# Weight conversions from the 24th step, batch 0's token mixer in four pieces, one matmul over zeros a step, and only batch 1 projected unsplit

## The chip, the cores and the metric

The kernel runs on one NeuronCore of one Trainium2 chip. The metric is the time that the device needs for one execution, in microseconds (us). Of several executions the median is taken. The engines are called PE (matrix multiplication), DVE (vector), ACT (scalar, activations), POOL (GpSimd) and SP, whose queue issues the DMAs.

## The reference

A linear attention with random features, over 8 batches, 8 heads, 576 tokens and 64 values a head, and behind it a mixer over tokens (rank 32) and a two-layer mixer over channels (512 to 2048 to 512). U, V and the two channel weights come as 64-bit floats.

```python
def phi(x):
    proj = np.einsum('bhsd,df->bhsf', x, w_phi)
    proj = proj - np.max(np.abs(proj), axis=-1, keepdims=True)
    return np.concatenate([np.exp(proj), np.exp(-proj)], axis=-1)
q_p, k_p = (phi(q), phi(k))
kv = np.einsum('bhsf,bhsd->bhfd', k_p, v)
z = np.sum(k_p, axis=2)
num = np.einsum('bhsf,bhfd->bhsd', q_p, kv)
den = np.einsum('bhsf,bhf->bhs', q_p, z)[..., None] + 1e-06
x = (num / den)                         # then (batch, seq, 512)

h = x.transpose(0, 2, 1) @ U @ V
u = x + h.transpose(0, 2, 1)
ch = np.maximum(u @ w_ch1, 0.0) @ w_ch2
return (u + ch).astype(np.float32)
```

## The kernel before, in words

**Attention by pairs.** A `Pair` is two heads of one batch, so there are 32 pairs, four to a batch. For each one k and q come in by DMA (`raw`, and the last 64 of the 576 tokens in `t_r`), PE transposes them (L282, L291), then k is projected in two halves (`project_k`), q in two halves (`project_q`), and the 64 last tokens apart (`project_k_tail`, `project_q_tail`). The features are two exponentials (L325, L326 for k; L337, L338 for q, whose maximum over partitions is taken on POOL, L335). `kv_tail` and `kv_main` build the sums over tokens in PSUM (L404, L411), L417 copies them out, `out_tail` and `out_main` multiply by q's features (L437, L450) and `normalize` divides (L424 to L429).

**Two ways to project.** An unsplit pair (`self.split` false; batches 0 and 1) multiplies 32-bit floats, each such matmul being two instructions on PE, and ACT copies the transposed tiles out (L300, L310). A split pair (batches 2 to 7) writes each number as a rounded high part and a rest: ACT casts the high part (L273), DVE subtracts for the rest (L274), PE multiplies in the faster format (L371, L394, L395), and for k the two results are added with a copy on ACT (L374) and an addition on DVE (L375).

**Mixers.** `Tokens` mixes over tokens: `split` (ACT L507, DVE L508) writes x as two parts, `down` multiplies by U (L521) into `pst`, `up` multiplies by V (L537) and adds to x (L538). A `Mixer` then handles 512 tokens: `transposes` (L553, parts on ACT L231 and DVE L232), and for each of 16 blocks f of the hidden layer `hidden(f)` (12 matmuls, L565, one PSUM bank, then `h_hi` on ACT L570 and `h_lo` on DVE L571) and `add(f)` (12 matmuls, L582). These 32 calls of a batch are its chunks. There is one mixer a batch, and a ninth for the 64 last tokens of all batches.

**Weights.** The 16 blocks of each channel weight are loaded as 64-bit words and converted, block by block, in `convert` (L137, L138, L140 on ACT; L141, L142 on DVE; a 64-bit integer addition on POOL, L146; scratch tile `w_ab`), then split into two parts (L223 on ACT, L224 on DVE). There are 32 such blocks: block 2f is of the first weight, 2f+1 of the second.

**The order.** The Python loop runs one pair behind the other, and a scheduler at build time may move instructions within what dependences allow. `step(fn)` issues one stage of a pair and then calls `pace.step()`: it counts the steps, issues the conversions that are due (`CONVERT`: from the first number on, all 32 by the second), and then either one piece of the first token mixer (`pieces`), or the share of mixer chunks that is due, or, while there are no chunks, two matmuls over zeros that keep PE going (`keep_busy`). Batch 0 fills the first 33 steps. Its pieces are made in `first_tokens`; after the last piece the 28 chunks (32 less `HELD`) are spread over the steps up to `BATCH`. `LOADS` says up to which block the words are loaded at each of the first seven pairs; these DMAs stand in SP's queue.

PSUM has three banks for the tag `at`, one for `ph` and four for `o`. In batch 0 the tiles that are asked for as `late` use the four banks of `o`; the unsplit `project_k` is among them, the split one uses `at`.

Of the kernel before, what the change touches and what calls it, by code (L numbers as in the profile page):

```python
# [25 lines left out]
def tile_kernel(  # L26
# [12 lines left out]
    nc = tc.nc  # L39
# [166 lines left out]
    def convert_block(i):  # L206
        f, n = divmod(i, 2)
        r = convert(words[f][n], f"w{n + 1}_{f}")
        if f < LAST:
            w = home.tile([P, 2, C], F32R, tag=f"w{n + 1}_{f}", name=f"w{n + 1}_{f}")  # L210
            split_w(r, w)
        elif n == 0:
            found[f] = r
            return
        else:
            w1_w, w = place(f, F32R, (2, C), f"w_{f}")
            split_w(found[f], w1_w)
            split_w(r, w)
            w1_t[f] = w1_w
        (w1_t, w2_t)[n][f] = w  # L220

    def split_w(r, w):
        nc.scalar.copy(out=w[:, 0, :], in_=r)  # L223
        nc.vector.tensor_sub(w[:, 1, :], r, f32(w[:, 0, :]))  # L224

    def w1_part(f, part, c):
# [5 lines left out]
        nc.vector.tensor_sub(dst_lo, src, f32(dst_hi))  # L232


    SPLIT = 2

    class Pair:


        def __init__(self, b, j):  # L240
            self.b, self.h0, self.nm = b, 2 * j, f"{b}_{j}"
            self.split = b >= SPLIT
            self.tail = slice((b % 2) * ST, (b % 2 + 1) * ST)
            nm, hs = self.nm, slice(self.h0, self.h0 + 2)
            self.raw = []
            for n, src in enumerate((k, q)):
                m = raw.tile([P, 2, NT // 2, 2 * D], F32, tag="raw", bufs=2, name=f"raw{nm}_{n}")
                self.loaded = nc.sync.dma_start(
                    out=m.rearrange("p h s e -> p h (s e)"),
                    in_=src[b, hs, 0:SM, :].rearrange("h (p t) d -> p h (t d)", t=NT))  # L250
                self.raw.append(m)

            self.t_r = raw.tile([P, 2 * D], F32, tag="t_r", bufs=1, name=f"t_r{nm}")
            for n, src in enumerate((k, q)):
                nc.sync.dma_start(
                    out=self.t_r[n * ST:(n + 1) * ST, :].rearrange("r (h d) -> r h d", h=2),
                    in_=src[b, hs, SM:S, :].rearrange("h r d -> r h d"))
# [388 lines left out]
    class Pace:  # L646
# [5 lines left out]
        def step(self):  # L652

            steps[0] += 1
            blocks((steps[0] - CONVERT[0]) * 2 * NFC // (CONVERT[1] - CONVERT[0]))
            if pieces:
                pieces.pop(0)()
                if not pieces:
                    self.chunks, self.steps = 32 - HELD, BATCH - steps[0]
                return  # L660
            n = (self.at + 1) * self.chunks // self.steps - self.at * self.chunks // self.steps
            self.at += 1
            mix(n)
            if not self.chunks:

                keep_busy(2, True)

# [3 lines left out]
    def keep_busy(n, here=False):  # L673
        wp = ps("busy", "ph")
        for _ in range(n):
            ins = nc.tensor.matmul(wp, zeros[:, 0:P], zeros, start=True, stop=True)
            if here:
                tc.keep_in_program_order(ins)

    LOADS = (1, 3, 6, 9, 12, 14, 15)  # L680
    CONVERT = (12, 62)
    BATCH = 67
    pieces = []
    HELD = 4
# [42 lines left out]
    def first_tokens(tk):  # L727
        m = []

        def begin():  # L730
            tk.up(2)
            tk.up(3)
            m.append(Mixer(tk.b, tk.x))
            m[0].transposes(0)

        def end():
            m[0].transposes(3)
            todo.extend(m[0].chunks())

        return [  # L740
            lambda: tk.split(1),
            lambda: tk.down(1),
            lambda: [tk.up(t) for t in range(2)],
            begin,
            lambda: [m[0].transposes(1), tk.up(NT)],
            lambda: m[0].transposes(2),
            end]

    if True:
        cur = Pair(0, 0)  # L750
        load_w_phi()
        cur.load_v()
        keep_busy(6)
        cur.transposes()
        cur.s_project_k0()
        cur.s_project_k1()
        cur.s_project_q0()
        nxt = Pair(0, 1)
        nxt.load_v()
        nxt.transposes()  # L760
        cur.s_kv0_q1()
        cur.s_kv1()
        x = home.tile([P, NT, C], F32, tag="w_last", name="x0")
        xt = moe.tile([P, C], F32, tag="xt", name="xt0")
        nc.vector.memset(xt[ST:P], 0.0)
        tk = Tokens(0, x, xt)
        for n, (b, j) in enumerate(pairs):

            far = Pair(*pairs[n + 2]) if n + 2 < len(pairs) else None
            if n < len(LOADS):  # L770

                with tc.issue_after(far.loaded.ins):
                    weights(LOADS[n])
            if far is not None:
                far.load_v()
            if nxt is not None:
                step(nxt.s_project_k0)
            step(cur.s_out0, x, xt)
            if nxt is not None:
                step(nxt.s_project_k1)  # L780
            step(cur.s_out1, x)
            if j == 1:
                tk.split(0)
            if j == NPAIR - 1:
                fill = []
                if nxt is not None:
                    fill = [nxt.s_project_q0, far.transposes, nxt.s_kv0_q1, nxt.s_kv1]
                if b == 0:
                    pieces.extend(first_tokens(tk))
                    for fn in fill:  # L790
                        step(fn)
                else:
                    tokens(tk, fill)
                    pace = Pace(32 - HELD, 34)
                if nxt is not None:
                    if b % 2 == 1:
                        xt = moe.tile([P, C], F32, tag="xt", name=f"xt{b + 1}")
                        nc.vector.memset(xt[ST:P], 0.0)
                    x = moe.tile([P, NT, C], F32, tag="x", name=f"x{b + 1}")
                    tk = Tokens(b + 1, x, xt)  # L800
            else:
                step(nxt.s_project_q0)
                if n == 0:
                    load_uv()
                if j == 1:
                    step(tk.down, 0)
                if far is not None:
                    step(far.transposes)
                step(nxt.s_kv0_q1)
                step(nxt.s_kv1)  # L810
            cur, nxt = nxt, far
        mix(len(todo) - HELD)
        x = moe.tile([P, NT, C], F32, tag="x", name="x_tail")
        nc.sync.dma_start(out=x, in_=u_dram[B])
        m = Mixer(B, x)
        for t in range(NT):
            m.transposes(t)
            mix()
        todo.extend(m.chunks())
        mix(len(todo))  # L820
# [31 lines left out]
```

## Time and profile before

| | |
|---|---|
| time, median of 3 runs | 1282.24 us (1282.2 to 1285.5) |
| the profiled execution | 1287.0 us, span of its instructions 1285.2 us |
| PE | 1252.3 us busy, 97% of the span |
| DVE | 643.4 us, 50% |
| ACT | 548.1 us, 43% |
| POOL | 202.9 us, 16% |

"Busy" is the time in which at least one instruction of the engine runs. The page's strip of the span in 40 slices shows where the engines differ: the shares of DVE and ACT are highest in the first seven slices (some 220 us), and the granted clock of PE is below full there alone.

```profile
DVE  5887665464555454555456455545455543211211
ACT  6788584444443444344343444344434431111110
PEclk9986899999999999999999999999999999999999
```

Five events of DVE mark the stages of the text below. A row of the timeline has the start, the time that the instructions took, the engine, line, operation, tiles, count, and in brackets the idle time before and what ended it.

```profile
94.98 0.76 DVE L508 TENSOR_TENSOR xs<-x,xs 128x256 fp32r<-128x256 f32 x2 [1.19 <-ACT xs L507]
...
122.04 0.68 DVE L232 TENSOR_TENSOR uT_lo<-pt,uT_hi 128x512 fp32r<-128x512 f32 x1
...
140.53 0.69 DVE L571 SCALAR_TENSOR_TENSOR h_lo<-ph,h_hi 128x512 fp32r<-128x512 f32 x1 [0.83 <-ACT h_hi L570]
...
181.18 0.69 DVE L571 SCALAR_TENSOR_TENSOR h_lo<-ph,h_hi 128x512 fp32r<-128x512 f32 x1
...
210.69 0.69 DVE L571 SCALAR_TENSOR_TENSOR h_lo<-ph,h_hi 128x512 fp32r<-128x512 f32 x1 [2.19 <-ACT h_hi L570]
```

The first is the start of the split of batch 0's last half of x, the second the last part of its transposed tokens, then come the 2nd, the 6th and the 9th `h_lo` of its mixer.

### The profile page before, as it was taken

What the parts mean: (1) busy time and instruction counts of PE and PEld (TensorE: products, weight loads), DVE (VectorE), ACT (ScalarE), POOL (GpSimd) and SP (SyncE); (2) the same over time, 40 slices, a digit from 0 to 9 for tenths busy, and PEclk for the clock granted to TensorE, in tenths of its full rate; (3) what the DMA queues carried; (4) which work ended last, traced back from release to release, by engine and by line L of the source; (5) the groups of instructions that cost most, each with busy time, mean ns of one, the idle gap of its engine ahead of it and who ended that gap; (6) DMA issues with size and microseconds to landing.
All of it is one profiled execution on the core that took longest, in us unless ns stands there. A gap on an engine that the chain in (4) does not pass through costs nothing.

```text
span 1285.2 us, 17973 instructions
## 1 busy us (share of the span) xinstructions
PE 1252.3 (97%) x6961; PEld 1071.5 (83%) x6968; DVE 643.4 (50%) x1425; ACT 548.1 (43%) x1167; POOL 202.9 (16%) x154
## 2 busy tenths in 40 slices
PE   9878999999999999999999999999999999999997
PEld 7656878888888888888888888888888888788886
DVE  5887665464555454555456455545455543211211
ACT  6788584444443444344343444344434431111110
POOL 3444352011110111111111111011111120000000
PEclk9986899999999999999999999999999999999999
DMA  6644321121113111210112111311121002100001
GB/s 192 204 140 148 93 61 35 50 76 27 30 47 111 28 29 45 78 61 25 47 47 75 28 30 47 111 29 28 45 77 61 21 1 86 66 1 1 33 1 33
DMA packets 90100, 75.38 MB, mean 59 GB/s; under 512 B 51488, under 2 KB 76448, under 8 KB 89888
## 3 DMA queue, kind: packets, MB, share of 16 engines
q1 hardware_dynamic: 90016, 74.24, 18.9%
q8 instruction: 55, 0.90, 0.3%
q14 instruction: 29, 0.24, 0.1%
HBM read 55.35 MB, written 18.87 MB: 58 GB/s over the span
## 4 chain that ended last, share of the span: by engine, by line
PE 89%; ACT 5%; DVE 3%; DMA 1%; issue 1%; SPq 0%; POOL 0%; DVEq 0%; ACTq 0%; POOLq 0%
PE o L582 30%; PE ph L565 30%; PE xp L450 8%; PE kv_ps L411 8%; PE T L291 2%; PE pk L371 2%; PE pp L521 1%; PE pt L553 1%; PE pq L394 1%; ACT w_ab L137 1%; PE kv_ps L404 1%; ACT w_ab L138 1%; PE xpt L437 1%; PE pq L395 1%; ACT w_ab L140 1%
## 5 line engine op out<-in xcount | busy, mean ns | idle before, releaser
L565 PE MATMUL ph<-uT_hi,w 128*128 128x512 f32 x1152 | 388.5, 396 | 1.1 <-ACT uT_hi L231 1.1
L582 PE MATMUL o<-w,h_hi 128*128 128x512 f32 x1152 | 330.4, 399 | 0.1
L565 PEld LDWEIGHTS ph<-uT_hi,w 128*128 128x128 f32 x1152 | 216.3, 189 | 44.7 <-ACT uT_hi L231 1.6
L582 PEld LDWEIGHTS o<-w,h_hi 128*128 128x128 f32 x1152 | 213.3, 190 | 41.9 <-issue 0.7
L571 DVE SCALAR_TENSOR_TENSOR h_lo<-ph,h_hi 128x512 fp32r<-128x512 f32 x144 | 99.2, 689 | 273.2 <-ACT h_hi L570 272.7
L565 PE MATMUL ph<-uT_lo,w 128*128 128x512 f32 x576 | 227.2, 394 | 0.5 <-DVE uT_lo L232 0.5
L570 ACT ACTIVATE h_hi<-ph 128x512 fp32r<-128x512 f32 x144 | 86.1, 598 | 323.4 <-PE ph L565 313.9
L582 PE MATMUL o<-w,h_lo 128*128 128x512 f32 x576 | 191.1, 396 | 0.0
L335 POOL PARTITION_ALL_REDUCE qp<-qp x64 | 128.1, 2002 | 386.4 <-ACT qp L334 375.2
L450 PEld LDWEIGHTS xp<-kv,qp 128*128 128x128 f32 x1024 | 125.7, 196 | 15.4 <-ACT qp L337 4.7
L450 PE MATMUL xp<-kv,qp 128*128 128x65 f32 x1024 | 127.1, 277 | 8.9 <-ACT qp L337 4.0
L565 PEld LDWEIGHTS ph<-uT_lo,w 128*128 128x128 f32 x576 | 108.7, 189 | 23.7 <-DVE uT_lo L232 2.6
L411 PEld LDWEIGHTS kv_ps<-vb,kp 128*128 128x128 f32 x1024 | 124.4, 196 | 3.6 <-issue 0.8
L411 PE MATMUL kv_ps<-vb,kp 128*128 128x65 f32 x1024 | 124.2, 276 | 0.1
L582 PEld LDWEIGHTS o<-w,h_lo 128*128 128x128 f32 x576 | 106.5, 188 | 20.9 <-issue 0.2
L274 DVE TENSOR_TENSOR T<-T,T 64x512 fp32r<-64x512 f32 x96 | 66.2, 689 | 84.7 <-ACT T L273 83.6
L273 ACT CAST T<-T 64x512 fp32r<-64x512 f32 x96 | 55.8, 581 | 97.8 <-PE pq L395 71.9
L335 POOL PARTITION_ALL_REDUCE qp_t<-qp_t x32 | 25.4, 794 | 381.0 <-ACT qp_t L334 380.8
L374 ACT COPY kp<-pk 128x256 f32<-128x256 f32 x96 | 35.6, 371 | 71.6 <-PE pk L371 71.4
L325 ACT ACTIVATE kp<-kp 128x512 f32<-128x512 f32 x64 | 40.4, 631 | 58.5 <-DVE kp L322 46.3
L375 DVE TENSOR_TENSOR kp<-pk,kp 128x256 f32<-128x256 f32 x96 | 40.2, 419 | 29.8 <-ACT kp L374 29.5
L336 DVE TENSOR_TENSOR qp<-qp 128x512 f32<-128x512 f32 x64 | 47.4, 740 | 11.6 <-POOL qp L335 11.0
(125 smaller groups left out, 1397.5 us busy)
## 6 DMA issues: line engine op xcount, KB each, us to landing
words<-in_moe_w_ch_dram SPq DMA_DIRECT2D x32, 512.0 KB, 6.7
raw<-in_k_dram SPq DMA_DIRECT2D x32, 256.0 KB, 2.8
raw<-in_q_dram SPq DMA_DIRECT2D x32, 256.0 KB, 3.0
vb<-in_v_dram SPq DMA_DIRECT2D x64, 128.0 KB, 2.6
u_dram<-x SPq DMA_DIRECT2D x32, 256.0 KB, 2.5
st<-u_dram SPq DMA_DIRECT2D x16, 512.0 KB, 4.4
out_dram<-st SPq DMA_DIRECT2D x32, 256.0 KB, 2.6
t_r<-in_k_dram SPq DMA_DIRECT2D x32, 32.0 KB, 2.2
```

Source lines behind the costliest of these rows:

```text
L273: nc.scalar.copy(out=dst[0:D], in_=src)
L274: nc.vector.tensor_sub(dst[D:2 * D], src, f32(dst[0:D]))
L325: nc.scalar.activation(out=kp[:, :, 0:F], in_=kp[:, :, F:2 * F], func=AF.Exp)
L335: nc.gpsimd.partition_all_reduce(qp[:, 0, :], qp[:, 1, :], P, ReduceOp.absmax)
L336: nc.vector.tensor_sub(qp[:, 1, :], qp[:, 1, :], qp[:, 0, :])
L375: nc.vector.tensor_tensor(out=k_w[:, ts_, :], in0=pk[:, :, 0, :], in1=kp[:, ts_, 0:F], op=ALU.add)
L411: nc.tensor.matmul(self.kv_v[:, f, g, :], kp[:, t, f * F:(f + 1) * F], self.vb[:, g, t, :], start=False, stop=(t == NT - 1), skip_group_ch ...
L450: nc.tensor.matmul(xv[:, c, :], qp[:, f, c * P:(c + 1) * P], self.kv[:, f, c // 2, :], start=(f == 0), stop=(f == 1))
L565: nc.tensor.matmul(ph, w1_part(f, l, c), r[:, c, :], start=(n == 0), stop=(n == 3 * NCC - 1))
L570: nc.scalar.activation(out=h_hi, in_=ph, func=AF.Relu)
L571: nc.vector.scalar_tensor_tensor(out=h_lo, in0=ph, scalar=0.0, in1=f32(h_hi), op0=ALU.max, op1=ALU.subtract)
L582: nc.tensor.matmul(self.o[t], l[:, cs], w2_t[f][:, r, :], start=(f == 0 and n == 0), stop=(f == NFC - 1 and n == 2))
```

## The change

Five things change. `CONVERT` goes from (12, 62) to (24, 63), and `LOADS` loads the words a pair later. The high part of the second weight's blocks is cast on DVE in place of ACT. `first_tokens` returns four pieces in place of seven, and the first of them is issued at once, ahead of the next step, so that the chunks start four steps earlier and are spread over 35 steps in place of 31. `keep_busy` is called for one matmul in place of two, and now also between the pieces. Batch 0 is projected split, so that batch 1 alone stays unsplit.

```diff
         if f < LAST:
             w = home.tile([P, 2, C], F32R, tag=f"w{n + 1}_{f}", name=f"w{n + 1}_{f}")
-            split_w(r, w)
+            split_w((nc.scalar.copy, nc.vector.tensor_copy)[n], r, w)
...
-            split_w(found[f], w1_w)
-            split_w(r, w)
+            split_w(nc.scalar.copy, found[f], w1_w)
+            split_w(nc.vector.tensor_copy, r, w)
...
-    def split_w(r, w):
-        nc.scalar.copy(out=w[:, 0, :], in_=r)
+    def split_w(copy, r, w):
+        copy(out=w[:, 0, :], in_=r)
         nc.vector.tensor_sub(w[:, 1, :], r, f32(w[:, 0, :]))
...
-    SPLIT = 2
+    UNSPLIT = 1
...
-            self.split = b >= SPLIT
+            self.split = b != UNSPLIT
...
                 if not pieces:
                     self.chunks, self.steps = 32 - HELD, BATCH - steps[0]
+                else:
+                    keep_busy(1, True)
                 return
...
             if not self.chunks:
-                keep_busy(2, True)
+                keep_busy(1, True)
...
-    LOADS = (1, 3, 6, 9, 12, 14, 15)
-    CONVERT = (12, 62)
+    LOADS = (-1, 1, 3, 6, 9, 12, LAST)
+    CONVERT = (24, 63)
...
             lambda: tk.split(1),
-            lambda: tk.down(1),
-            lambda: [tk.up(t) for t in range(2)],
-            begin,
-            lambda: [m[0].transposes(1), tk.up(NT)],
-            lambda: m[0].transposes(2),
-            end]
+            lambda: [tk.down(1)] + [tk.up(t) for t in range(2)],
+            lambda: [begin(), m[0].transposes(1), tk.up(NT)],
+            lambda: [m[0].transposes(2), end()]]
...
                     pieces.extend(first_tokens(tk))
+                    pieces.pop(0)()
```

Line numbers behind the edits are one higher in the changed kernel from L233 on, and three higher from about L670 on. Three places of the built order show what moves.

On DVE, from the copy of the second pair's sums (`kv_1`) on, the third pair's k is projected (`pk`, `kp`; `mk` is the maximum). Before:

```order
L417 COPY kv_1_483<-kv_ps_1_453 128x260
L142 TENSOR_SCALAR v_ab<-v_ab 128x64
L320 TENSOR_REDUCE mk_2_0_519<-pk_0_2_515 128x4
L322 TENSOR_TENSOR kp_2_0_518<-pk_0_2_515,mk_2_0_519 128x4x128
L336 TENSOR_TENSOR qp_1_1_466<-qp_1_1_466 128x512
```

Now:

```order
L418 COPY kv_1_525<-kv_ps_1_495 128x260
L321 TENSOR_REDUCE mk_2_t<-pkt_2_548 128x1
L337 TENSOR_TENSOR qp_1_1_509<-qp_1_1_509 128x512
L323 TENSOR_TENSOR kp_2_t<-pkt_2_548,mk_2_t 128x128
L376 TENSOR_TENSOR kp_2_0_557<-pk_0_2_558,kp_2_0_557 128x2x128
L376 TENSOR_TENSOR kp_2_0_557<-pk_0_2_563,kp_2_0_557 128x2x128
L321 TENSOR_REDUCE mk_2_0_568<-kp_2_0_557 128x4
```

The two additions of the split projection (L376) stand ahead of the maximum, each on a PSUM tile of its own, where before the maximum read PSUM at once.

On ACT, behind the last exponential of the third pair's first half of q, the conversions of the weights (`w_1_ab` and on; `words` are what was loaded) stood in a block ahead of the fourth pair's features. Before:

```order
L338 ACTIVATE qp_2_0_605<-qp_2_0_605 128x512
L137 ACTIVATE w_1_ab<-words_1_276 128x512
L138 ACTIVATE w_1_ab<-words_1_276 128x512
L140 ACTIVATE w_1_ab<-words_1_276 128x512
L524 CAST pst_614<-pp_0_615 128x256
L137 ACTIVATE w_1_ab<-words_2_277 128x512
L138 ACTIVATE w_1_ab<-words_2_277 128x512
L140 ACTIVATE w_1_ab<-words_2_277 128x512
L137 ACTIVATE w_2_ab<-words_1_495 128x512
L138 ACTIVATE w_2_ab<-words_1_495 128x512
L140 ACTIVATE w_2_ab<-words_1_495 128x512
L325 ACTIVATE kp_3_t<-kp_3_t 128x128
```

Now:

```order
L339 ACTIVATE qp_2_0_659<-qp_2_0_659 128x512
L375 COPY kp_3_0_774<-pk_0_3_775 128x2x128
L326 ACTIVATE kp_3_t<-kp_3_t 128x128
L375 COPY kp_3_0_774<-pk_0_3_780 128x2x128
L327 ACTIVATE kp_3_t<-kp_3_t 128x128
L375 COPY kp_3_1_818<-pk_0_3_819 128x2x128
L375 COPY kp_3_1_818<-pk_0_3_824 128x2x128
```

The fourth pair's features follow at once, with the copies of the split projection (L375) among them.

On DVE, from the eighth `h_lo` of the first mixer on, before:

```order
L571 SCALAR_TENSOR_TENSOR h_lo_7_1943<-ph_7_1929,h_hi_7_1942 128x512
L424 TENSOR_SCALAR den_2_1_1994<-xp_1_2_1985 128x4
L336 TENSOR_TENSOR qp_3_t<-qp_3_t 128x128
L425 RECIPROCAL den_2_1_1994<-den_2_1_1994 128x4
L429 TENSOR_TENSOR x_1208<-xp_1_2_1985,den_2_1_1994 128x2x2x64
L274 TENSOR_TENSOR tail_T_0_2047<-tT_0_2045,tail_T_0_2047 64x2x64 x2
L571 SCALAR_TENSOR_TENSOR h_lo_8_2012<-ph_8_1998,h_hi_8_2011 128x512
```

Now, the rows from a little behind the eighth up to the ninth:

```order
L141 TENSOR_SCALAR w_14_ab<-w_14_ab 128x512
L430 TENSOR_TENSOR xt_295<-xpt_2_1979,den_2_t_1986 64x64
L430 TENSOR_TENSOR x_1253<-xp_1_2_1990,den_2_0_1999 128x2x2x64
L142 TENSOR_SCALAR w_14_ab<-w_14_ab 128x512
L141 TENSOR_SCALAR w_15_ab<-w_15_ab 128x512
L142 TENSOR_SCALAR w_15_ab<-w_15_ab 128x512
L224 TENSOR_TENSOR w_14_2311<-w_14_ab,w_14_2311 128x512
L321 TENSOR_REDUCE mk_3_1_2024<-pk_1_3_2020 128x4
L223 CAST w_14_2363<-w_14_ab 128x512
L572 SCALAR_TENSOR_TENSOR h_lo_8_2017<-ph_8_2003,h_hi_8_2016 128x512
```

Before, the conversions were over by the eighth `h_lo`; now those of the last blocks stand behind it, the cast of a second weight's block (L223) among them.

## The prediction

> **What bounds the kernel now.** I read the windows view first, cut where the first batch hands over to its mixer (the five DVE rows stand in the section on the profile): at 95.0 us the split of the last half of x begins (the 6th `xs` subtraction, L508), at 122.0 the fourth `uT_lo` stands (L232), at 140.5, 181.2 and 210.7 the 2nd, 6th and 9th `h_lo` (L571) of the first mixer. A row gives the stretch and its length, then busy us with instruction counts of PE, PE's weight loads, DVE, ACT and POOL, the granted clock, the DMA share and GB/s.
>
> ```profile
> 0.00:22.00 22.00, 19.65 (x101) 14.87 (x102) 9.40 (x25) 12.89 (x28) 7.55 (x21) 1.00 0.64 192
> 22.00:95.00 73.00, 61.01 (x388) 48.02 (x393) 60.09 (x138) 58.47 (x128) 34.38 (x27) 0.95 0.56 176
> 95.00:122.00 27.00, 21.81 (x101) 18.34 (x102) 20.22 (x41) 22.66 (x44) 11.84 (x7) 0.70 0.55 181
> 122.00:140.50 18.50, 17.11 (x58) 12.68 (x57) 17.02 (x31) 13.54 (x27) 10.41 (x8) 0.71 0.02 4
> 140.50:181.20 40.70, 40.70 (x246) 35.34 (x244) 20.01 (x47) 26.58 (x52) 11.75 (x9) 1.00 0.32 97
> 181.20:210.70 29.50, 27.02 (x131) 21.90 (x130) 23.88 (x47) 22.23 (x44) 13.41 (x9) 0.94 0.12 35
> 210.70:1285.20 1074.50, 1065.01 (x5948) 920.36 (x5945) 492.77 (x1101) 391.68 (x848) 113.54 (x73) 1.00 0.15 45
> ```
>
> From 210.7 on PE is busy 99% at full clock, and nothing there is edited. Time can come or go only ahead of that. There PE stands still, or has a clock of 0.70, because DVE and ACT are full: DVE is busy 92% of the fourth row (17.02 of 18.50). The same stretches, with only the instructions that touch a conversion's scratch tile `w_ab` (DVE, ACT, POOL, then clock and DMA), show whose work that is:
>
> ```profile
> 22.00:95.00 73.00, 22.70 (x33) 27.24 (x44) 15.22 (x11) 0.95 0.56 176
> 95.00:122.00 27.00, 8.75 (x15) 16.68 (x27) 6.73 (x5) 0.70 0.55 181
> 122.00:140.50 18.50, 12.57 (x15) 8.24 (x14) 6.66 (x5) 0.71 0.02 4
> 140.50:181.20 40.70, 6.49 (x13) 12.72 (x20) 6.69 (x5) 1.00 0.32 97
> 181.20:210.70 29.50, 15.65 (x20) 14.40 (x24) 8.56 (x6) 0.94 0.12 35
> ```
>
> Conversions are nearly half of ACT's work from 22 to 95 us, and two thirds of DVE's between 181 and 211, where PE loses 2.5 us and some clock.
>
> **The change, part by part.** The rows of a group are line, engine, operation, tiles, count, busy us and mean ns, then idle time before it. First the projection of batch 0, which becomes split (24 pairs ran split before, 8 unsplit).
>
> ```profile
> L371 PE MATMUL pk<-w_hl,T 128*128 128x256 f32 x192 | 39.7, 289 | 0.0
> L394 PE MATMUL pq<-T,w_hl 128*128 128x512 f32 x48 | 21.4, 445 | 0.0
> L395 PE MATMUL pq<-T,w_hl 128*128 128x512 f32 x48 | 18.8, 392 | 0.0
> L356 PE MATMUL pk<-w_two,T 128*128 128x256 f32 x64 | 18.8, 421 | 3.4 <-DVE den_t L425 2.3 <-ACT T L300 1.0
> L397 PE MATMUL pq<-T,w_two 128*128 128x512 f32 x32 | 18.3, 666 | 0.8 <-DVE kv L417 0.5 <-DVE den_t L425 0.3
> L274 DVE TENSOR_TENSOR T<-T,T 64x512 fp32r<-64x512 f32 x96 | 66.2, 689 | 84.7 <-ACT T L273 83.6
> L274 DVE TENSOR_TENSOR tail_T<-tT,tail_T 64x128 fp32r<-64x128 f32 x48 | 13.9, 290 | 13.9 <-ACT tail_T L273 13.1
> L375 DVE TENSOR_TENSOR kp<-pk,kp 128x256 f32<-128x256 f32 x96 | 40.2, 419 | 29.8 <-ACT kp L374 29.5
> L273 ACT CAST T<-T 64x512 fp32r<-64x512 f32 x96 | 55.8, 581 | 97.8 <-PE pq L395 71.9 <-DVE T L274 12.5 <-PE T L291 9.4
> L374 ACT COPY kp<-pk 128x256 f32<-128x256 f32 x96 | 35.6, 371 | 71.6 <-PE pk L371 71.4
> L300 ACT COPY T<-T 128x512 f32<-128x512 f32 x16 | 9.2, 586 | 3.2 <-PE pq L397 1.9 <-PE T L291 1.3
> ```
>
> PE: split (39.7+21.4+18.8)/24 = 3.33 us a pair, unsplit (18.8+18.3)/8 = 4.64; four pairs save 5.2 us. DVE gains (66.2+13.9+40.2)/24 = 5.01 us a pair, 20.1 in all. ACT gains 55.8/24 + 35.6/24 - 9.2/8 = 2.66 a pair, 10.6 in all. POOL loses a memset a pair, hidden either way.
>
> Next the conversions and the matmuls over zeros.
>
> ```profile
> L137 ACT ACTIVATE w_ab<-words 128x512 uint16<-128x512 uint16 x32 | 25.0, 782 | 3.9 <-PE pp L521 3.2 <-DVE w L224 0.7
> L138 ACT ACTIVATE w_ab<-words 128x512 f16<-128x512 f32 x32 | 24.4, 761 | 0.0
> L140 ACT ACTIVATE w_ab<-words 128x512 f32<-128x512 f32 x32 | 20.7, 648 | 0.0
> L223 ACT CAST w<-w_ab 128x512 fp32r<-128x512 f32 x32 | 19.2, 616 | 4.3 <-POOL w_ab L146 4.2
> L141 DVE TENSOR_SCALAR w_ab<-w_ab 128x512 f32<-128x512 f32 x32 | 20.7, 647 | 14.9 <-ACT w_ab L140 14.8
> L142 DVE TENSOR_SCALAR w_ab<-w_ab 128x512 int32<-128x512 int32 x32 | 18.2, 570 | 0.5
> L224 DVE TENSOR_TENSOR w<-w_ab,w 128x512 fp32r<-128x512 f32 x32 | 28.7, 906 | 3.5 <-ACT w L223 3.3
> L142 DVE TENSOR_SCALAR v_ab<-v_ab 128x512 int32<-128x512 int32 x1 | 0.4, 427 | 0.0
> L180 DVE CAST v_all<-v_ab 128x512 fp32r<-128x512 f32 x1 | 0.8, 804 | 0.0
> L676 PE MATMUL busy<-zeros 128*128 128x512 bf16 x57 | 19.2, 418 | 1.5 <-DVE zeros L671 1.2
> L137 ACT ACTIVATE u_ab<-u_st 128x160 uint16<-128x160 uint16 x1 | 0.4, 387 | 1.6 <-DMA u_st<-in_moe_U_dram 1.6
> ```
>
> A block costs ACT 89.3/32 = 2.79 us and DVE 67.6/32 = 2.11. For a `w_ch2` block the 0.62 us cast leaves ACT for DVE. Of that copy the trace has one example of its size, 0.80 us beside POOL work; a one-input operation of the size took 0.43 alone. I take 0.57, the mean of the 32 like it, between these ends. The matmuls over zeros fall from 64 to 37: 27 x 19.2/57 = 9.1 us of PE.
>
> Now by stage, with the conversions counted in the built order.
>
> Up to 95.0 us DVE has 9.40 + 60.09 = 69.5 us. Off go 22.7 of conversions, on come 20.1 of split, and the order keeps four blocks here, two of them with the new cast: 4 x 2.11 + 2 x 0.57 = 9.6. That makes 76.5. ACT comes to 71.4 - 27.2 + 10.6 + 9.9 = 64.7, so **DVE takes ACT's place as the bound of batch 0**. DVE can do little before the first transposes:
>
> ```profile
> 5.49 1.71 PE T L291 x8
> ```
>
> With 5.5 us of lead and DVE at 92%, the share of the stage that it limits now, the stage takes 5.5 + 76.5/0.92 = 88.7: **-6.3**. At 96% it would be 85.2 (-9.8), at 80% 101.1 (+6.1). The 5.2 and 9.1 us of PE all lie in this stage, beside DVE; I cost them at nothing. If DVE is no cover, they count. SP's queue has the first 2 MB of weight words behind U and V instead of ahead of them, which ends the 1.6 us wait for `u_st`; DVE's load hides that too.
>
> 95.0 to 122.0: the order has seven conversions on ACT with two casts, 7 x 70.1/32 + 2 x 0.6 = 16.5 us, against 16.68. The four pieces in place of seven change nothing that I can find: the first hidden matmul stands at the same place of the attention as before. **0**, with -4 as the end if fewer casts free PE's clock, +3 if not.
>
> 122.0 to 140.5: in the order DVE gets, by lines L141, L142, L224 and L223, 5, 7, 7 and 3 operations: 3.2 + 4.0 + 6.3 + 1.7 = 15.2 us against 12.57. (17.02 + 2.6)/0.92 = 21.3: **+2.8**.
>
> 140.5 to 181.2: PE is busy throughout, conversions become fewer. **0**.
>
> 181.2 to 210.7: before, the clump of conversions cost PE 29.50 - 27.02 = 2.5 us of standing still, and the mean clock 0.94 is 12% at half speed, 1.8 us: 4.3. The change leaves more blocks for this place: between the 6th and the 9th `h_lo` stand eleven, six casts with them, 11 x 2.11 + 6 x 0.57 = 26.6 us against 15.65. Scaled by that, the loss is 7.3: **+3.0**. Its ends are 0, if PE finds other rows to run, and +8.4, if DVE's 34.8 us at 92% (37.8) set the whole stage.
>
> After 210.7: nothing, beyond a conversion or two that PE's 1065 us hide.
>
> **Sum**: -6.3 + 2.8 + 3.0 = -0.5. The profiled execution took 1287.0 us (a span of 1285.2 and 1.8 around it), 4.8 above the median 1282.24; the forecast is 1286.5 for a run like it, and 1281.7 against the median. Under 0.3% (3.8 us) counts as no change.
>
> **Rivals.** (1) The later clumps are hidden: in the fifth row PE did not stand still at all beside 12.7 us of conversions on ACT. Then only batch 0's gain is left: 1282.2 - 6.3 = 1275.9. Against it: the sixth row, where they did cost. (2) PE is what limits batch 0 (80.7 busy of 95 us), and its 5.2 + 9.1 us come off one for one: 1267.9. Against it: these 95 us hold 18 of matmuls over zeros, put where PE waits. (3) **Slower**: the split projection passes its results through three PSUM banks (the tag `at`), where the unsplit one of batch 0 used the other four as well; a bank is free only when ACT and then DVE have read it, so DVE's queue runs dry between pairs. At 80% the first stage is 101.1 and the sum +11.9: 1294. It decides from where DVE fills less than 87% of that stage (5.5 + 76.5/0.87 = 93.4: -1.6 + 5.8 = +4.2). (4) **Slower by the clock**: with half of the zeros gone the clock falls inside batch 0.
>
> ```profile
> 84.49 0.44 PE L450 MATMUL xp<-kv,qp 128*128 128x65 f32 x2 [4.00 <-ACT qp L337]
> 120.65 2.05 PE L356 MATMUL pk<-w_two,T 128*128 128x256 f32 x4 [2.33 <-DVE den_t L425]
> 85.00:90.00 5.00, 3.18 (x15) 3.18 (x16) 4.50 (x9) 3.91 (x10) 2.10 (x2) 0.51 0.01 3
> 120.00:125.00 5.00, 4.27 (x9) 3.00 (x10) 4.92 (x13) 3.98 (x7) 1.76 (x2) 0.50 0.01 3
> ```
>
> A wait of PE of 4.00 us was followed by half clock, and so was one of 2.33. The stage would hold 80.7 - 5.2 - 9.1 = 66 us of PE work in 88.7; if 45% of that work ran at half speed (a mean clock of 0.70, as in the third row, is 60% of the time) it would be 95.7, which makes the sum +0.7 + 5.8 = +6.5: 1288.7. The Trainium skill ("TensorE: Matmul & The Clock Gate", "HAM oscillation") allows idle gaps up to about 3.4 us before the clock halves, and would see only the first of these two waits as a danger; the second row differs, and the trace decides. By the page's gap the sum would have nothing to add here as long as DVE feeds PE every few us.
>
> **How the numbers follow.** Forecast 0.33; rival 1 0.23; 2 0.13; 3 0.21; 4 0.10. So faster by over 0.3% 0.36, within 0.33, slower 0.31. The forecast's own range is 1278.4 to 1286.1. The range of 1268 to 1294 reaches to rivals 2 and 3 and leaves out some 0.2 beyond them.
>
> **What would show it.** In the new profile: the 6th `xs` subtraction at about 89 us with DVE near 92% busy up to it; the fourth `uT_lo` 27 us later; the 2nd `h_lo` at about 137; a stretch of some 30 to 38 us between the 6th and 9th `h_lo` with DVE full and PE standing still 5 us or more; the clock at 1.00 up to 85 us. A first stage over 93 us means rival 3 (clock 1.00) or 4 (clock below). PE waiting nowhere after 140 us means rival 1.

## The result, and the profile after

The changed kernel takes 1299.78 us (median of 4 runs, 1298.01 to 1306.83), the one before 1282.22 (4 runs). The ratio is 1.0153, with a 95% interval of 1.0129 to 1.0177: **slower by 1.5%, and beyond the upper end of the range**. The profiled execution took 1306.83 us (span 1304.9); against the profiled execution before that is 19.7 us more in the span. It is the slowest of the four, 7.0 us above their median, so the stages below add up to more than the medians' 17.6.

The page's strip of 40 slices, the changed kernel, the three rows that were shown of before:

```profile
DVE  6788668464545554564555455455455543211211
ACT  5579567444444444434453444344444441111110
PEclk8688897999999999999999999999999999999999
```

ACT is lighter in the first three slices and in the sixth, and heavier in the fourth and the seventh. The clock dips in the first five slices and in the seventh, where before it did in the third to the fifth. The windows view of the changed kernel, cut at the same five events (6th `xs` subtraction, fourth `uT_lo`, 2nd, 6th and 9th `h_lo`), with the columns of the prediction:

```profile
0.00:99.40 99.40, 85.29 (x453) 74.01 (x454) 72.69 (x182) 62.69 (x146) 30.98 (x37) 0.79 0.45 134
99.40:123.10 23.70, 18.14 (x114) 14.00 (x113) 19.68 (x43) 22.50 (x46) 10.88 (x7) 0.98 0.73 233
123.10:146.10 23.00, 17.13 (x70) 13.32 (x70) 21.55 (x41) 17.72 (x34) 13.03 (x10) 0.80 0.18 56
146.10:180.10 34.00, 34.00 (x179) 28.99 (x178) 17.83 (x40) 15.43 (x31) 5.78 (x5) 0.95 0.24 82
180.10:224.30 44.20, 39.14 (x183) 33.19 (x183) 37.26 (x66) 34.14 (x63) 22.10 (x16) 0.81 0.29 92
224.30:1304.90 1080.60, 1069.25 (x5947) 922.48 (x5946) 499.03 (x1115) 396.71 (x859) 117.72 (x76) 0.99 0.15 45
```

| stage, up to | before, us | forecast | after |
|---|---|---|---|
| 6th `xs` | 95.0 | -6.3 | 99.4 (+4.4) |
| 4th `uT_lo` | 27.0 | 0 | 23.7 (-3.3) |
| 2nd `h_lo` | 18.5 | +2.8 | 23.0 (+4.5) |
| 6th `h_lo` | 40.7 | 0 | 34.0 (-6.7) |
| 9th `h_lo` | 29.5 | +3.0 | 44.2 (+14.7) |
| the end | 1074.5 | 0 | 1080.6 (+6.1) |

Up to the 6th `xs` DVE is busy 72.69 of 99.40 us, 73% and not 92%. A mean clock of 0.79 over 99.4 us is 2 x 0.21 x 99.4 = 42 us at half speed (I reckon half clock in this way below). The views of waits of the changed kernel show PE and DVE waiting for each other (total, times, longest, in us); the first row is PE from 10 to 75 us, the other two DVE from 24 to 95:

```profile
PE kv_ps L405 <- DVE tail_T L275: 4.0, 1, 4.0
...
DVE kv L418 <- PE kv_ps L412: 6.6, 2, 4.3
DVE mk_t L321 <- PE pkt L349: 2.5, 1, 2.5
```

The 4.0 us end at 40.7. Four windows of five us each from there on show the clock at half:

```profile
40.00:45.00 5.00, 4.32 (x21) 4.35 (x21) 4.16 (x8) 0.00 (x0) 0.20 (x1) 0.53 0.68 244
45.00:50.00 5.00, 5.00 (x24) 4.91 (x24) 1.04 (x3) 1.82 (x4) 1.94 (x1) 0.50 0.12 26
50.00:55.00 5.00, 5.00 (x25) 4.82 (x24) 3.44 (x13) 3.37 (x8) 0.00 (x0) 0.50 0.13 30
55.00:60.00 5.00, 5.00 (x24) 4.81 (x24) 3.21 (x10) 3.52 (x9) 0.56 (x1) 0.50 0.00 0
```

By the profile PE is busy without a gap from 45 to 60, yet the clock stays at half. The Trainium skill ("TensorE: Matmul & The Clock Gate", "Part 1: The HAM clock gate") gives full rate back after about 3.4 us of sustained work; these 15 us, which the profile shows as busy, differ.

### The profile page after: what moved, and what is told of

Same layout as the page of the kernel before. It is cut to its first block, busy times and chain, and to the rows that moved or that the text cites. A ratio compares the mean times of both kernels' runs of the same rounds, so it can differ in the third digit from the quotient of the medians.

```text
span 1304.9 us, 17976 instructions
## 1 busy us (share of the span) xinstructions
PE 1262.9 (97%) x6939; PEld 1086.0 (83%) x6941; DVE 668.0 (51%) x1481; ACT 549.2 (42%) x1175; POOL 200.5 (15%) x150
## 4 chain that ended last, share of the span: by engine, by line
PE 90%; DVE 6%; ACT 2%; issue 1%; DMA 0%; POOL 0%; SPq 0%; DVEq 0%; POOLq 0%; ACTq 0%
PE ph L566 30%; PE o L583 30%; PE xp L451 8%; PE kv_ps L412 8%; PE pk L372 2%; PE T L292 2%; PE pp L522 1%; PE kv_ps L405 1%; PE pq L395 1%; DVE w L224 1%; PE xpt L438 1%; PE pq L396 1%; PE pt L554 1%; DVE w_ab L141 1%; PE vp L538 1%
## 5 line engine op out<-in xcount | busy, mean ns | idle before, releaser
L412 PEld LDWEIGHTS kv_ps<-vb,kp 128*128 128x128 f32 x1024 | 130.0, 203 | 5.0 <-issue 2.0
L451 PEld LDWEIGHTS xp<-kv,qp 128*128 128x128 f32 x1024 | 128.5, 200 | 5.0 <-issue 1.0
L412 PE MATMUL kv_ps<-vb,kp 128*128 128x65 f32 x1024 | 129.7, 283 | 1.0 <-ACT kp L327 1.0
L275 DVE TENSOR_TENSOR T<-T,T 64x512 fp32r<-64x512 f32 x112 | 77.0, 689 | 83.7 <-ACT T L274 82.0
L274 ACT CAST T<-T 64x512 fp32r<-64x512 f32 x112 | 65.1, 582 | 101.9 <-PE pq L396 72.7
L336 POOL PARTITION_ALL_REDUCE qp_t<-qp_t x32 | 26.1, 816 | 409.6 <-ACT qp_t L335 396.0
L375 ACT COPY kp<-pk 128x256 f32<-128x256 f32 x112 | 41.4, 372 | 87.2 <-PE pk L372 79.6
L376 DVE TENSOR_TENSOR kp<-pk,kp 128x256 f32<-128x256 f32 x112 | 46.5, 419 | 35.9 <-ACT kp L375 35.3
L372 PE MATMUL pk<-w_hl,T 128*128 128x256 f32 x224 | 51.9, 318 | 3.6 <-DVE pst L526 1.9
```

Source lines behind the costliest of these rows:

```text
L274: nc.scalar.copy(out=dst[0:D], in_=src)
L275: nc.vector.tensor_sub(dst[D:2 * D], src, f32(dst[0:D]))
L336: nc.gpsimd.partition_all_reduce(qp[:, 0, :], qp[:, 1, :], P, ReduceOp.absmax)
L372: nc.tensor.matmul(pk[:, i, :, :], self.T[0][:, i, cs], w_hl, start=True, stop=True)
L375: nc.scalar.copy(out=kp[:, ts_, 0:F], in_=pk[:, :, 1, :])
L376: nc.vector.tensor_tensor(out=k_w[:, ts_, :], in0=pk[:, :, 0, :], in1=kp[:, ts_, 0:F], op=ALU.add)
```

## The experiments

Ratios are to the kernel before on the same chip. With each edit the scheduler placed the whole program anew, so an edit's price holds what moved with it on other engines as well: in u_fill, which adds nothing but matmuls, DVE's and ACT's order differs from some 28 us on. "6th `xs`" is the end of batch 0's stage in the profiled execution. The rows are windows from the start to that event, in the columns above.

### First: one part undone at a time

**u_conv**: the schedule of conversions and loads of before.

```diff
-    LOADS = (-1, 1, 3, 6, 9, 12, LAST)
-    CONVERT = (24, 63)
+    LOADS = (1, 3, 6, 9, 12, 14, 15)
+    CONVERT = (12, 62)
```

> The change with its conversions and loads put back to the schedule of before (12, 62). Theory A, the clump: of the 19.7 us that the changed kernel lost, 14.7 lie between the 6th and the 9th h_lo, where VectorE spends 26.6 us on conversions; put back, this stage returns from 44.2 to about 30 us, and the time from 1299.8 to 1284 to 1288. Theory B, the clock: the half-clock stretches of batch 0 (24.3 to 99.4 us at a granted clock of 0.76) and of the later stages come from the missing zeros and the thin matmul work and stay; the time falls by less than 7 us, to no lower than 1293. A third outcome that both leave room for: conversions back in the first two dozen steps fill VectorE there again and the 6th xs comes later than 99.4.

1303.32 us (1.0175, 1.0154 to 1.0196): no gain. The stage to the 9th `h_lo` fell to 39.2 us, but the 6th `xs` came at 105.0, with DVE busy for 88.95 us:

```profile
0.00:105.00 105.00, 84.16 (x438) 70.39 (x441) 88.95 (x204) 73.63 (x165) 38.90 (x43) 0.80 0.52 159
```

That is the third outcome of the expectation, and Theory A, as I had put it, falls: with the early schedule back the late stage is 5.0 us shorter, the first one 5.6 longer, and nothing is gained.

**u_split**: batch 0 unsplit again.

```diff
-            self.split = b != UNSPLIT
+            self.split = b > UNSPLIT
```

> The change with batch 0 projected unsplit again, as before. Theory C, the split: it makes the matmuls of batch 0 shorter and puts a second half-width eviction and its wait into each projection, so it costs batch 0 its 4.4 us and more; undone, the 6th xs comes at 92 to 95 us instead of 99.4 and the time is 1290 to 1296. Theory B, the clock: with the longer unsplit matmuls TensorE is busier, and the half clock between 40.3 and 64.2 us goes; the same sign, but then the granted clock of 24.3 to 99.4 us rises from 0.76 above 0.85. Theory A, the clump: nothing after the 6th xs moves, the stage between the 6th and the 9th h_lo keeps its 44 us, so no lower than 1293.

1280.79 us (1.0000, 0.9990 to 1.0009): the whole loss is gone, more than any theory gave it. Its windows, to the 6th `xs` and from the 6th to the 9th `h_lo`:

```profile
0.00:74.80 74.80, 68.51 (x447) 56.11 (x448) 53.14 (x143) 53.19 (x120) 31.76 (x41) 1.00 0.59 175
...
155.10:198.70 43.60, 36.28 (x166) 29.99 (x166) 36.59 (x60) 33.76 (x62) 20.56 (x14) 0.84 0.29 94
```

The 6th `xs` came at 74.8, 20 us ahead of before, at full clock. The late stage kept its 43.6 us. So the change held a large gain, a large loss in the same stage, and a second loss later.

**u_fill**: two matmuls over zeros a step.

```diff
-                    keep_busy(1, True)
+                    keep_busy(2, True)
...
-                keep_busy(1, True)
+                keep_busy(2, True)
```

> The change with two matmuls over zeros a step instead of one. Theory B, the clock: the half-clock stretches (about 78 us in all against 37.5 before) shrink by half, which gives back up to 15 us of TensorE's time, and the time falls to 1288 to 1293. Theory A and C, the clump and the split: the waits stay as they are, the zeros only fill them; within 3 us of 1299.8.

1290.20 us (1.0068, 1.0045 to 1.0090): 9.6 us back, within Theory B's range. The mean clock up to the 6th `xs` (95.1) rose from 0.79 to 0.91, some 25 us less at half, and that stage gained 4.3 us. More came where no zeros run, from the 6th to the 9th `h_lo`:

```profile
170.40:203.50 33.10, 28.61 (x157) 24.88 (x155) 26.45 (x44) 25.47 (x48) 16.93 (x11) 0.91 0.37 122
```

That is 11.1 us less than the changed kernel's 44.20. DVE's work on `w_ab` in this stage is 18.3 us where the changed kernel has 26.6: the new order left more conversions for later, where 4.7 us come back. So the 9.6 us are not the price of the clock alone.

**u_cast**: all casts of weights on ACT.

```diff
-            split_w((nc.scalar.copy, nc.vector.tensor_copy)[n], r, w)
+            split_w(nc.scalar.copy, r, w)
...
-            split_w(nc.vector.tensor_copy, r, w)
+            split_w(nc.scalar.copy, r, w)
```

> The change with all high-part casts of the weights on ScalarE again, as before. On VectorE 16 such casts took 613 ns each, 9.8 us in all, of which about half stands in the stage between the 6th and the 9th h_lo, where VectorE is busy 37.3 of 44.2 us. Theory A with VectorE as the bound there: the stage shortens by about 5 us, to 1294 to 1296. Theory A with the chain across ScalarE, VectorE and GpSimd as the bound: ScalarE, busy 34.1 of 44.2 us, takes them with no gain; 1297 to 1303. Theory B: no change, within 2 us of 1299.8.

1289.68 us (1.0076, 1.0061 to 1.0091): 10.1 us back, more than either form of Theory A gave. The stage to the 9th `h_lo` fell from 44.2 to 36.8; the 6th `xs` moved from 99.4 to 96.2.

### Second: one part alone, and the rest without the split

**b_conv**: before, with the change's `LOADS` and `CONVERT` (the first diff, the other way round).

> The kernel before with the late conversions and loads alone. In the run of the change with batch 0 unsplit the 6th xs came at 75.2 us (95.4 before) and the stage between the 6th and the 9th h_lo took 43.6 us (29.5 before), 1280.8 in all. Theory D, the two halves of the conversions' move: they give batch 0 about 20 us and take 14 back at h_6 to h_9 and 6 behind: 6th xs at 75 to 80, that stage 36 to 44, time 1272 to 1283. Theory A as first stated, the clump alone: batch 0 gains less than 8 us and the time is 1285 to 1292. If the second zeros matter for the clock in h_6 to h_9 (half clock 6.3 us there with two zeros, 17.4 with one), the stage is near 36 and the time near 1272.

1266.54 us (0.9889, 0.9872 to 0.9907): **faster than both kernels by more than 14 us**. Its windows, the first and the last three of the six stages:

```profile
0.00:75.50 75.50, 70.89 (x465) 58.29 (x466) 51.15 (x141) 54.26 (x122) 31.56 (x41) 1.00 0.60 179
...
124.60:162.50 37.90, 37.90 (x212) 32.05 (x211) 22.47 (x52) 27.33 (x55) 13.90 (x11) 1.00 0.43 133
162.50:191.70 29.20, 27.02 (x138) 21.85 (x137) 26.52 (x51) 26.50 (x53) 17.23 (x12) 1.00 0.27 86
191.70:1265.00 1073.30, 1062.83 (x5932) 918.01 (x5930) 497.03 (x1107) 394.10 (x853) 114.82 (x74) 1.00 0.15 45
```

Batch 0's stage lost 19.5 us, with DVE's busy time down by 69.5 - 51.2 = 18.3. From the 6th `xs` to the end it is 1265.0 - 75.5 = 1189.5 us against 1190.2 before: seven more conversions behind batch 0 cost nothing, with the casts on ACT. The half of Theory D that took these 20 us back later is wrong.

**b_split**: before, with batch 0 split.

```diff
-            self.split = b >= SPLIT
+            self.split = b != 1
```

> The kernel before with batch 0 projected split alone. Theory C, the split: it costs batch 0 some 20 us, of which half clock is a part: the 6th xs comes at 110 to 116 us and the time is 1298 to 1305; by the stage before that the conversions overlap with it. Theory B, the clock: with two zeros a step batch 0 shows less than 20 us of half clock and the split costs 5 to 10 us, 1287 to 1292. If the split costs only beside late conversions, the time stays within 4 us of 1282.

1292.08 us (1.0088, 1.0068 to 1.0107). 10.7 us, the upper end of Theory B's time; the 6th `xs` came at 104.8 with 0.89 of the clock (23 us at half, where B had under 20). DVE's work rose by 17.0 us to 86.50, the stage by 9.8:

```profile
0.00:104.80 104.80, 87.83 (x489) 70.42 (x490) 86.50 (x201) 79.06 (x177) 39.84 (x44) 0.89 0.52 160
```

**b_fill**: before, with one matmul over zeros.

```diff
-                keep_busy(2, True)
+                keep_busy(1, True)
```

> The kernel before with one matmul over zeros a step instead of two. Theory B, the clock: half clock enters the first 75 us, which had none, and the time rises by 3 to 10 us. Against it: with unsplit projections and one zero the run of the change with batch 0 unsplit had no half clock before 75.2 us, so 27 zeros less leave the clock as it is and each saves its 0.4 us where TensorE is the bound: 1270 to 1282.

1282.58 us (1.0008, 0.9991 to 1.0025): no change, on the edge between the two. Half clock up to the 6th `xs` (93.0) rose to 2 x 0.09 x 93 = 17 us, while the stage came 2.0 us earlier. That the zeros saved pay for the clock is likely, and not shown.

**us_cast**: the change with batch 0 unsplit and all casts on ACT (the diffs of u_split and u_cast together).

> The change with batch 0 unsplit and all casts of weights on ScalarE: what is left of the change is the late conversions, the four pieces and the one matmul over zeros. The stage from the 6th to the 9th h_lo took 43.6 us with batch 0 unsplit alone and 36.8 us with the casts on ScalarE alone. If the two add, the stage is 36 to 38 us and the time 1270 to 1275, below both kernels. If the casts were worth something only because half clock (37.5 against 41.0 us in batch 0) changed with them, the time stays at 1278 to 1283.

1265.95 us (0.9885, 0.9865 to 0.9904), as fast as b_conv, from which it differs by the four pieces and the one matmul over zeros: these are together worth nothing here. It is below both forecasts. Without the split, casts on DVE cost 1280.79 - 1265.95 = 14.8 us. Its windows as for u_split:

```profile
0.00:74.60 74.60, 69.00 (x452) 57.21 (x452) 52.30 (x140) 54.44 (x123) 32.38 (x41) 1.00 0.58 176
...
149.70:186.00 36.30, 34.46 (x190) 29.64 (x189) 30.21 (x57) 34.53 (x64) 19.08 (x13) 0.95 0.36 112
```

### Third: what in the split, the casts and the zeros

**u_bank**: the change with the split k results in the four `o` banks.

```diff
-            pk = self.ps(f"pk{g}{s}_").rearrange(
+            pk = self.ps(f"pk{g}{s}_", True).rearrange(
```

> The change, with the half-width results of the split k projection of batch 0 written to the banks that batch 0's unsplit projection uses (tag o) instead of the three at banks. Theory C1, the banks: TensorE's waits in batch 0 come from too few free at banks, and the 6th xs moves from 99.9 towards 80 us, the time to 1282 to 1290. Theory C2, the chain of the split projection (copy of the low part, add, maximum, subtraction, two exponentials, in place of four of these) or the clock alone: the banks were free, and the time stays within 4 us of 1299.8.

1286.96 us (1.0044, 1.0023 to 1.0066): 12.8 us back by the medians, but its 10 runs reach from 1284.15 to 1295.03 and the profiled one is the slowest. There the 6th `xs` came at 95.4 at the same clock, 0.79: batch 0's stage did not move towards 80, so C1 fails. From the 6th to the 9th `h_lo` it has the 33.1 us of u_fill, with the same work on DVE (26.45 us). So most of what came back lies where the edit changes nothing but the order, and that the banks have a part in it isn't shown.

**u_k**: the change with batch 0's main k projections unsplit.

```diff
-            if self.split:
+            if self.split and self.b:
                 return self.project_k_split(g)
...
-                if self.split:
+                if self.split and (n or self.b):
                     m = att.tile([P, 2, SM], F32R, tag=f"T{n}", name=f"T{n}_{nm}")
```

> The change with batch 0's four main k projections unsplit; its q projections and its tails stay split. Of the 24 us that the split costs in batch 0 beside late conversions (6th xs 75.0 with batch 0 unsplit against 96.6 split, both with the casts on ScalarE), theory C2, the longer chain of the k projection that ends in waits of TensorE and in half clock, gives back most: 6th xs below 85 us, 1280 to 1288. If the work of VectorE and ScalarE for both operands is what counts, about half comes back: 6th xs at 86 to 92, 1288 to 1294. If the half clock is set off by the first pair's tail (waits at 17.1 and 36.7 us before the half clock of 19.8 and 40.3), which stays split, nothing comes back: 1296 to 1303.

1281.94 us (1.0006, 0.9992 to 1.0019): 17.8 of the 19.0 us that u_split gave back. It is the main k projection; the split of q and of the tails costs next to nothing in the time, though the 6th `xs` comes 4.6 us later than in u_split.

```profile
0.00:79.40 79.40, 70.50 (x450) 59.31 (x451) 60.23 (x158) 54.52 (x124) 30.31 (x37) 0.96 0.57 171
```

**us_memset**: us_cast, with a fill on DVE that is overwritten.

```diff
             w = home.tile([P, 2, C], F32R, tag=f"w{n + 1}_{f}", name=f"w{n + 1}_{f}")
+            if n:
+                nc.vector.memset(f32(w[:, 1, :]), 0.0)
             split_w(nc.scalar.copy, r, w)
```

> The version with the late conversions, four pieces, one matmul over zeros, batch 0 unsplit and all casts on ScalarE (1265.95 us), with a fill of 128x512 elements put on VectorE for each w2 block where the change has its cast; the fill is overwritten and waits for no GpSimd result. With the casts on VectorE this version takes 1280.8. Theory E1, VectorE's time: the fills cost about what the casts do, 1276 to 1282. Theory E2, the wait: a cast on VectorE waits for GpSimd's addition at the head of VectorE's queue and holds all behind it, a fill does not: 1265 to 1270.

1279.95 us (0.9983, 0.9963 to 1.0004; 10 runs from 1273.49 to 1283.00): 14.0 us, nearly what the casts cost, and so within E1: work on DVE costs as much without a wait for POOL at the head of its queue. The groups of DVE show how much work, the fill here and the cast in the changed kernel:

```profile
L212 DVE MEMSET w<- 128x512 f32 x15 | 7.3, 485 | 0.8
```

```profile
L223 DVE CAST w<-w_ab 128x512 fp32r<-128x512 f32 x16 | 9.8, 613 | 3.9 <-POOL w_ab L146 3.9
```

Either costs more than its own 7.3 or 9.8 us. They need not cost it in the same way. The cast's row has 3.9 us of waiting for POOL, which the fill's lacks. And against us_cast the casts' loss lies from the 6th to the 9th `h_lo` (43.6 us in u_split for 36.3), where the fill adds only 2.3 (its profiled execution, at 1275.68 us, is 4.3 below the median):

```profile
155.70:194.30 38.60, 34.52 (x190) 28.32 (x188) 33.73 (x64) 36.45 (x68) 19.50 (x13) 0.98 0.34 106
```

So it is shown that such work costs 14 us without the wait, and not that the wait has no part in the casts' price.

**us_f0**: us_cast with no zeros in the steps (both calls of `keep_busy(1, True)` taken out).

> The version with the late conversions, four pieces, batch 0 unsplit and all casts on ScalarE (1265.95 us with one matmul over zeros a step), with none. Some 33 such matmuls of 0.38 to 0.45 us, 12 to 15 us, leave the first 75 us. If TensorE's full clock there holds by itself with unsplit projections and TensorE is the bound: 6th xs at 62 to 68 us, 1255 to 1262. Theory B, the clock: without zeros the waits are bare, half clock enters the first 75 us for 15 us and more, and the 6th xs stays at 72 to 82 us: 1263 to 1275.

1272.74 us (0.9929, 0.9910 to 0.9948): 6.8 us more than with one. Theory B holds here:

```profile
0.00:82.20 82.20, 72.48 (x423) 61.57 (x423) 53.22 (x141) 54.61 (x122) 31.53 (x41) 0.88 0.55 165
```

DVE's and ACT's work is that of us_cast within 1 us and PE has 29 matmuls less, but the clock is 0.88 (20 us at half) and the stage 7.6 us longer.

### Fourth: work or clock in batch 0

**u_late**: the change, conversions from the 33rd step (`CONVERT = (33, 63)`).

> The change with conversions from the 33rd step on instead of the 24th: the seven that stood in batch 0 come after it, its split projection stays. VectorE's work up to the 6th xs falls from 80 to about 60 us, what it is with batch 0 unsplit (59 us, 6th xs at 75.2). Theory F, VectorE's work sets batch 0: the 6th xs comes at 76 to 84 us instead of 99.9. Theory G, the chain of the split projection and the clock: TensorE waits in the same places and 30 us and more of half clock stay, 6th xs at 90 to 97. The seven conversions come back behind batch 0 in either case and cost up to 15 us there, so the time is 1290 to 1300 by F and 1298 to 1312 by G.

1285.70 us (1.0038, 1.0022 to 1.0053), below both forecasts; the 6th `xs`, at 89.6, lies between them.

```profile
0.00:89.60 89.60, 79.63 (x449) 69.12 (x450) 61.34 (x169) 53.24 (x130) 24.61 (x33) 0.81 0.48 146
```

DVE's work fell by 11.4 us, not 20, as four conversions left the stage and not seven, and the stage by 9.8. By that slope it is Theory F; but with as much DVE work as u_k (60.2 and 61.3) it is 10.2 us longer, at 34 us of half clock against 6: that speaks for G. Neither theory alone covers it.

**u_late_f**: the same with two matmuls over zeros (the diff of u_fill).

> The same with two matmuls over zeros a step. Theory F: half clock in batch 0 was a by-effect, the zeros cost what they take where TensorE has no room: 6th xs within 3 us of the run with one. Theory G: half clock in batch 0 falls below 18 us, and the 6th xs comes 5 to 12 us earlier than with one, or stays where the zeros' own 8 to 10 us take the gain back. The time 5 to 10 us below that with one.

1289.95 us (1.0075, 1.0050 to 1.0100), slower than with one. The clock rose to 0.90 and the 6th `xs` came 2.6 us earlier (87.0); the stage to the 9th `h_lo` went from 35.4 to 43.6 us, which neither theory had. As between the changed kernel and u_fill, the order differs there: DVE's work on `w_ab` in that stage is 26.1 us with two zeros and 20.4 with one. Why the scheduler places it so wasn't followed up.

**u_cast_f**: the change, casts on ACT and two matmuls over zeros.

> The change with all casts on ScalarE and two matmuls over zeros: what is left is the late conversions, the four pieces and the split. Casts alone gave back 10.1 us, the second zeros alone 9.6. If the two are separate prices: 1278 to 1283. If both gave back the same half clock in the stages behind batch 0: 1287 to 1291.

1285.68 us (1.0029, 1.0010 to 1.0048): between the two. The second zeros give 4.0 us beside ACT's casts, 9.6 beside DVE's; part of what the two edits give back is the same.

**b_late**: before, with the change's `LOADS` and `CONVERT = (30, 67)`.

> The kernel before with the loads of the change and conversions from the 30th to the 67th step, later than the change's 24th to 63rd. With the 24th it took 1266.5 us. If each of the seven conversions left in batch 0 costs it 2.8 us (19.5 us for the seven that the 24th step took out of it) and costs less behind it: 1255 to 1265. If TensorE sets batch 0 by now (busy 52 of 56 us in the run with batch 0 unsplit) and the conversions crowd h_5 to h_8: 1267 to 1280.

1267.21 us (0.9879, 0.9859 to 0.9900), no better than b_conv and the lower end of the second forecast. The 6th `xs` came at 72.0, 3.5 us earlier for 8 us less of DVE work. PE is busy 66.91 of the 72.00 us, so little more can be gained there by DVE.

```profile
0.00:72.00 72.00, 66.91 (x456) 55.32 (x456) 43.14 (x127) 45.01 (x105) 25.80 (x37) 1.00 0.59 176
```

## Why the prediction was wrong

One ladder of medians sums it up: before 1281.4 (the runs beside them); late conversions 1266.5; four pieces and one zero besides 1266.0; casts on DVE 1280.8; the split 1299.8. Two terms of the sum were mis-sized. The first failed by **DVE's busy time turned into time by a share of 92%**, borrowed from one stage (122.0 to 140.5 us); the second by **a loss of PE scaled with the conversions**.

**Up to the 6th `xs` (-6.3, was +4.4).** "5.5 + 76.5/0.92 = 88.7" had the work about right: 72.69 us after against 76.5. What it had wrong is the rest, the time in which DVE is not busy: I took 88.7 - 76.5 = 12.2 us, and it was 99.4 - 72.7 = 26.7. It could be read before: 95.0 - 69.5 = 25.5. The same formula gives 5.5 + 69.5/0.92 = 81.0 for the kernel before, which took 95.0. So -6.3 is a reckoned stage less a measured one; reckoned on both sides it would have been +7.6, and the sum +13.4 in place of -0.5.

In the runs the time without DVE stays between 16 and 29 us (u_conv 16.1, b_split 18.3, u_k 19.2, us_cast 22.3, b_conv 24.4, u_late 28.3, b_late 28.9, us_f0 29.0) while the work goes from 43 to 89. So the stage is better described as DVE's work plus a wait than as work over a share; 76.5 + 25.5 would have given 102. The conversions' 18 us come off one for one, as b_conv shows, and beside late conversions the split puts them back: DVE's 20.1 was 70.57 - 52.30 = 18.3 (u_cast less us_cast), the stage 96.2 - 74.6 = 21.6. Beside early ones it adds 9.8 for 17.0 (b_split), so the wait is no constant. Nor does the description say which engine bounds the stage: PE is busy 69.00 of us_cast's 74.60 us. The row for u_cast:

```profile
0.00:96.20 96.20, 82.57 (x451) 70.14 (x453) 70.57 (x180) 63.35 (x147) 30.77 (x37) 0.80 0.46 136
```

DVE did pass ACT (72.69 us of work against 62.69); as ACT's 71.36 us went down with DVE's, which of them had held batch 0 before isn't told apart.

**122.0 to 140.5 (+2.8, was +4.5).** Here the share held, 21.55 of 23.00 us or 94%; DVE had 21.55 us of work where I counted 19.6.

**181.2 to 210.7 (+3.0, was +14.7).** I scaled PE's loss of 4.3 us to 7.3. By the same reckoning the changed kernel lost 44.20 - 39.14 = 5.1 us of standing still and 0.19 x 44.2 = 8.4 by the clock, 13.5 in all: that is the mis-sized term, and the clock is most of it. The other 5.5 us of the +14.7 go with matmuls that moved here: the order ran fewer up to the 6th `h_lo` (179 against 246) and more up to the 9th (183 against 131). The mechanism named at the upper end, DVE setting the whole stage at 92%, isn't shown: DVE was busy 37.26 of 44.20 us, 84%, and PE 39.14. In us_cast DVE has 83%, while PE (34.46 of 36.30) and ACT (34.53) are nearly full. But DVE's work counts: with the casts on ACT it falls by 6.1 us with the split (u_cast) and by 6.4 without (us_cast), the stage by 7.4 and 7.3. Nor did I see that moving the copies alone is worth 14.8 us, where their 9.8 us are about all that DVE has more: the difference is not settled, though the clock is part of it (0.84 in u_split's row, 0.95 in us_cast's).

**95.0 to 122.0 (0, was -3.3).** This is near the -4 that the prediction gave for a freer clock, and the clock is 0.98 where it was 0.70.

**140.5 to 181.2 (0, was -6.7).** It ran 67 matmuls fewer, so this gain and the loss behind it belong together: the two stages took 8.0 us more.

**After 210.7 (0, was +6.1).** PE has as many matmuls (5947 and 5948) and needs 4 us more for them, at 0.99. us_cast has such a tail too (1080.1) and is fast all the same; it wasn't followed up.

**Rivals.** By the prediction's own sign, a first stage over 93 us with the clock below full, it was Rival 4, the clock: I gave its stage 95.7 us, and 42 us of the 99.4 ran at half. How I read it, it is both cause and effect: PE waits for the longer k chain, slows, and DVE waits for PE. us_f0 has the clearest price: 7.6 us for 20 us of half clock, net of the zeros saved. It is not the whole loss: u_fill, left with 17 us of half clock, still needs 95.1 us to the 6th `xs`. Rival 3 had size and stage (101.1 forecast, 99.4 seen) and the low share of DVE, but not its cause: u_bank left the stage at 95.4 and 0.79, while u_k took it to 79.4. What stays open is how the 24.6 us of the split (99.4 - 74.8) divide into work and clock: between u_late, whose slope gives the 19.6 us of added DVE work nearly one for one, and u_k, against which u_late has 10 us that work does not explain. Rival 1, later clumps that are hidden, fails by the 44.2 us of their stage. Rival 2 fails by b_fill: zeros taken out were not time taken out.

## What to carry to other kernels

Try a formula for a stage on the kernel before first. The share taken from another stage gave 81.0 us for a stage that took 95.0, and set against the measured time it turned a loss into a forecast of -6; read the idle time in that very stage and keep it as a term of its own (work + wait). A bundle of edits should be taken apart before it is judged: one of these five alone is worth -14.8 us, and two others cost 33.8. Where a scheduler places the program anew, look where an edit's gain lies: of u_fill's and u_bank's, most lay in a stage that the edit does not touch. And where work is moved behind a stage, busy shares alone do not say which engine has room: seven more conversions cost nothing with the copies on ACT, nearly full there, and nearly 15 us with them on DVE.

## What the runs showed of the hardware

PE's clock stayed at half through windows in which PE was busy without a gap (45 to 60 us of the changed kernel). In us_f0 a wait of 3.55 us stood before such a stretch (a row of PE's timeline, then the window behind it):

```profile
37.53 1.23 PE L438 MATMUL xpt<-kv,qp_t 128*128 128x130 f32 x4 [3.55 <-DVE kv L418]
```

```profile
37.00:50.50 13.50, 12.97 (x51) 11.48 (x52) 8.45 (x26) 8.63 (x20) 1.22 (x2) 0.50 0.18 43
```

What a matmul over zeros is worth beside its 0.4 us has no one price here: the first one a step saved 6.8 us (us_f0, whose 6th `xs` came 7.6 us later), the second nothing in before (b_fill), 9.6 in the change, and it cost 4.3 in u_late_f, the last two with a changed order in a later stage that has no zeros.
